# Memory-recurrent attention with an FFN: token-stationary passes of 32 slots, weights streamed in four column groups

## The chip, the cores and the metric

The kernel runs on one core of a Trainium2 chip. The metric is the device time of one execution in microseconds (us), and lower is better. A program on one core is called "fast" when its run lies within 1.5% of the fastest run of the same kernel; a kernel that was run only once has the state "unknown".

The engines are named as in the profile: PE is the matmul engine (PEld its weight loads, which overlap with it), DVE the vector engine, ACT the scalar engine, POOL the general one, SP the one that issues most transfers. A "pair" is one weight load and the matmul that uses it. The stationary operand is the one that the weight load puts into the array; the other one moves through it.

## The reference

A sequence of 2048 tokens of width 640 is normalised and goes through attention in 64 segments of 32 tokens. Each segment attends to itself and to 8 memory slots, and the memory's own outputs are the memory of the next segment. An FFN with a hidden width of 1728 follows, both with residuals. There are 32 heads of width 128, and all data is bf16.

```python
mem = mem0                                   # 8 x 640
for s in range(64):                          # S = 2048, seg_len = 32
    xs = x[:, s * 32:(s + 1) * 32, :]        # x is layernormed
    h = concatenate([mem, xs], axis=1)       # 40 tokens
    q, k, v = (einsum('btd,dhe->bhte', h, W) for W in (Wq, Wk, Wv))      # 32 heads of 128
    scores = einsum('bhqe,bhke->bhqk', q, k) * scale
    scores = where(mask, scores, -1e9)       # mask[q, k] = (q < 8) or (q >= k)
    o = einsum('bhqk,bhke->bhqe', softmax(scores), v)
    o = einsum('bhte,hed->btd', o, Wo)
    mem = o[:, :8, :]                        # the recurrence
    outs.append(o[:, 8:, :])
h = x + concatenate(outs, axis=1)
gate, up = LN(h) @ W_gate, LN(h) @ W_up
return h + ((relu(gate) * up) @ W_down)      # cut: casts
```

By the mask the 8 memory queries see all 40 keys, and the token queries see the memory and the tokens up to their own.

## The kernel before

Everything in the recurrence is feature-major: the weights are stationary, and the 40 tokens of a segment (8 memory slots and 32 tokens) move. One head's projection is five pairs of 128 x 128 weights and 40 moving columns.

```python
for kind, payload in pe_ops:                       # (cut) the program of PE for one segment
    if kind == "tile":                             # 96 of them: V, Q, K of 32 heads
        ...
        for c in range(DC):                        # DC = 5
            mm = pe.matmul(outap, Wqkvv[:, j, c, h * Dh:(h + 1) * Dh], abuf[:, c, :],
                           start=(c == 0), stop=(c == DC - 1))
    ...                                            # "tg" transposes V, "sg" scores and mask,
    ...                                            # "sumpv" sums by a matmul with ones, and PV
    elif kind == "wo":                             # 160 pairs: output projection
        for pair in pairs:
            for h in range(H):
                ...
                for c in pair:
                    mm = pe.matmul(outap, Wov[:, h, c * 128:(c + 1) * 128],
                                   oTv[:, h * L:(h + 1) * L], start=(h == 0), stop=(h == H - 1))
```

The memory of the next segment is copied straight from the output projection's accumulators into the next segment's input, because the layout is the same:

```python
v.tensor_copy(anext[:, 0:5:2, 0:M], memE)
v.tensor_copy(anext[:, 1:5:2, 0:M], memO).then_inc(s_actrdy.h, 1)
```

The start-up loads x transposed, and only then the weights. It normalises all of x and stores it in a scratch buffer in device memory, from where each segment loads its tokens. At the end, the hidden state goes through scratch a second time before the FFN.

```python
def sync_start(sp):
    for b in range(NBLK):
        for c in range(DC):
            sp.dma_start(xT_blk[b][:, c, :], x_ap[b * TB:(b + 1) * TB, c * 128:(c + 1) * 128],
                         transpose=True).then_inc(s_x.h, 16)
def pool_weights(pool):
    pool.wait_ge(s_x.h, X_ALL)
    ...                                            # Wv, Wq, Wk, Wo, 5 MB each
def sync_store_pack(sp, b=b, c_pack_done=c_pack_done):
    sp.wait_ge(s_dln.h, c_pack_done)
    dst = scr_in[b * NSB:(b + 1) * NSB, :, :].rearrange("s p f -> p s f")
    ...
```

The softmax here doesn't subtract the row's maximum and nothing guards it: scores larger than these inputs give would overflow.

## Time and profile before

The median of the first three runs was 2047.39 us (2047.12 to 2047.9). The head of the profile's page gives the span, the busy time of each engine with its share and its count of instructions, and, for the queue that brings the engines' instructions, packets, megabytes and share of the transfer engines' time:

```profile
span 2047.5 us, 101764 instructions
PE 1771.0 (86%) x48661; PEld 1513.0 (74%) x48661; DVE 434.1 (21%) x927; ACT 653.1 (32%) x1185; POOL 8.0 (0%) x17
q8 instruction: 383, 6.28, 1.2%
```

The next view gives the busy times by stretches that I chose: start-up, recurrence, the passage to the FFN, and the FFN. Its columns are the stretch, its length, the busy time and count of each engine, the mean clock that the throttle granted to PE (1 is full speed), and the transfers' share and rate.

```profile
core 0: us, PE busy (x) PEld busy (x) DVE busy (x) ACT busy (x) POOL busy (x), PEclk, DMA share, GB/s
0.00:118.00 118.00, 15.99 (x45) 4.61 (x45) 28.51 (x69) 20.73 (x21) 7.96 (x17) 0.67 0.68 245
118.00:1755.00 1637.00, 1537.80 (x47488) 1409.27 (x47488) 326.19 (x702) 579.20 (x1088) 0.00 (x0) 0.93 0.05 9
1755.00:1796.00 41.00, 8.52 (x20) 2.33 (x21) 8.44 (x23) 7.91 (x7) 0.00 (x0) 0.55 0.74 227
1796.00:2047.00 251.00, 208.65 (x1110) 96.81 (x1108) 70.92 (x133) 45.30 (x69) 0.00 (x0) 0.94 0.03 11
```

Four fifths of the time is the recurrence, and PE is busy for 94% of it, with 742 matmuls a segment (47488 / 64) in 25.6 us. The timeline of one segment, cut to four lines, shows what these are. Its columns are start, duration from the first start to the last end, engine, line and operation, operands, sizes, and the count of instructions that were merged into the line; in brackets stands an idle time just before, and what ended it.

```profile
1000.50 1.69 PE L574 MATMUL ps_all<-act_70,Wqkv 128*128 128x40 bf16 x60
1008.23 4.93 PEld L650 LDWEIGHTS ps_all<-oTs,Wo_sb 128*128 128x128 bf16 x160
1008.23 5.03 PE L650 MATMUL ps_all<-oTs,Wo_sb 128*128 128x40 bf16 x160
1013.92 2.70 PE L574 MATMUL ps_all<-act_71,Wqkv 128*128 128x40 bf16 x100 [0.66 <-DVE act_71 L716]
```

Sixty pairs take 1.69 us, of which 0.18 us is the last matmul's own duration (the mean of one in the profile's groups), so 1.51 us / 59, about 26 ns a pair; 160 take 5.03 us, or 30 ns a pair. The wait for the hand-over of the memory is 0.66 us in the last line. Going by the FFN's matmuls of 512 columns, 0.215 us each, 40 columns would need about 17 ns (an estimate), less than a pair takes. PE is therefore bound by the number of pairs, each with few moving columns.

The chain of waits, in order of time, shows two places outside the recurrence. Its columns are start, duration and what it was:

```profile
41.80 41.54 DMA scr_in<-pack
1755.95 21.71 DMA hTb_85<-scr_h
```

The first store of normalised x to scratch lasted 41.5 us, beside the weights' loads, and the loads of the hidden state for the FFN came 21.7 us after the recurrence.

### The profile page before, as it was taken

Reading aid. Unit: us, or ns where it says so; the run is one execution under the profiler, and the core shown is the slowest. Engines: PE = TensorE matmul, PEld = TensorE weight load, DVE = VectorE, ACT = ScalarE, POOL = GpSimd, SP = SyncE. Lnnn points to the kernel's source line nnn. Section 1 sums busy time; section 2 is a strip of 40 time slices with the busy share of each in tenths; the row PEclk is TensorE's granted clock in tenths of the full one; section 3 lists DMA queues with packets and bytes.
Section 4 is the critical chain, followed back from the end, with each engine's and each line's share of the span. In section 5 each row is a group of like instructions: output and inputs, shape, how many; then the busy total and the mean of one; then the engine's idle time right before and its main releaser. Section 6 shows DMA issues by size and latency. Waiting matters only on the chain.

```text
span 2047.5 us, 101764 instructions
## 1 busy us (share of the span) xinstructions
PE 1771.0 (86%) x48661; PEld 1513.0 (74%) x48661; DVE 434.1 (21%) x927; ACT 653.1 (32%) x1185; POOL 8.0 (0%) x17
## 2 busy tenths in 40 slices
PE   2069999999999999999999999999999999387898
PEld 0068888888888888888888888888888888233344
DVE  1221111122111112222111111111111111133222
ACT  2123333333333333333333333333333333231111
POOL 1000000000000000000000000000000000000000
PEclk8579999999999999999999999999999999688999
DMA  6720000000000000000000000000000000500000
GB/s 215 302 55 9 8 9 9 8 9 9 9 8 9 9 9 8 9 9 8 9 9 9 9 9 9 8 9 9 9 9 9 9 8 8 170 13 13 14 13 14
DMA packets 96619, 55.11 MB, mean 27 GB/s; under 512 B 80008, under 2 KB 91984, under 8 KB 94288
## 3 DMA queue, kind: packets, MB, share of 16 engines
q1 hardware_dynamic: 91136, 26.98, 5.7%
q0 software_dynamic: 3008, 20.97, 2.5%
q8 instruction: 383, 6.28, 1.2%
q10 hardware_dynamic: 2064, 0.66, 0.1%
q14 instruction: 28, 0.23, 0.0%
HBM read 35.48 MB, written 10.49 MB: 22 GB/s over the span
## 4 chain that ended last, share of the span: by engine, by line
PE 79%; ACT 6%; DVE 5%; issue 4%; DMA 4%; SPq 1%; ACTq 0%; DVEq 0%
PE ps_all L574 41%; PE ps_all L650 14%; PE ps_all L589 7%; PE ps_all L979 3%; PE ps_all L982 3%; DMA scr_in<-pack 3%; PE ps_all L1048 3%; PE ps_all L603 3%; ACT L_sb L520 3%; PE ps_all L620 2%; PE ps_all L606 2%; ACT E_sb L510 1%; PE ps_all L629 1%; SPq L291 1%; DMA hTb_85<-scr_h 1%
## 5 line engine op out<-in xcount | busy, mean ns | idle before, releaser
L502 ACT ACTIVATE qkvT<-ps_all 128x480 bf16<-128x480 f32 x512 | 291.2, 569 | 849.6 <-PE ps_all L574 844.2
L574 PE MATMUL ps_all<-act_70,Wqkv 128*128 128x40 bf16 x15360 | 432.9, 180 | 40.4 <-DVE act_70 L716 20.3
L574 PEld LDWEIGHTS ps_all<-act_70,Wqkv 128*128 128x128 bf16 x15360 | 406.3, 96 | 71.6 <-issue 34.0
L574 PE MATMUL ps_all<-act_71,Wqkv 128*128 128x40 bf16 x15360 | 431.9, 180 | 20.9 <-DVE act_71 L716 20.9
L574 PEld LDWEIGHTS ps_all<-act_71,Wqkv 128*128 128x128 bf16 x15360 | 405.4, 96 | 52.2 <-DVE act_71 L716 24.3
L650 PE MATMUL ps_all<-oTs,Wo_sb 128*128 128x40 bf16 x10240 | 323.0, 192 | 1.8
L650 PEld LDWEIGHTS ps_all<-oTs,Wo_sb 128*128 128x128 bf16 x10240 | 312.8, 105 | 7.7 <-DVE oTs L698 5.2
L688 DVE COPY vtok<-ps_all 40x1024 bf16<-40x1024 bf16 x256 | 174.8, 683 | 459.4 <-PE ps_all L589 459.4
L698 DVE TENSOR_TENSOR oTs<-ps_all,r_sb 128x480 bf16<-128x480 f32 (+1 forms) x192 | 115.7, 603 | 615.9 <-ACT r_sb L528 615.9
L589 PE MATMUL ps_all<-ident,qkvT 128*40 128x128 bf16 x2048 | 160.1, 221 | 0.0
L510 ACT ACTIVATE E_sb<-ps_all 40x480 bf16<-40x480 f32 (+1 forms) x192 | 98.7, 514 | 135.2 <-PE ps_all L606 135.2
L520 ACT ACTIVATE L_sb<-ps_all 128x480 f32<-128x480 f32 (+1 forms) x192 | 100.6, 524 | 74.7 <-PE ps_all L620 74.7
L589 PEld LDWEIGHTS ps_all<-ident,qkvT 128*40 128x40 bf16 x2048 | 116.0, 99 | 9.4
L620 PE MATMUL ps_all<-E_sb,ones_bf 40*128 40x480 bf16 (+1 forms) x192 | 68.7, 358 | 54.7 <-ACT E_sb L510 51.5
L528 ACT ACTIVATE r_sb<-L_sb 128x480 bf16<-128x480 f32 (+1 forms) x192 | 107.2, 558 | 6.1
L629 PEld LDWEIGHTS ps_all<-E_sb,vtok 40*128 40x128 bf16 x2048 | 80.1, 94 | 13.8
L603 PE MATMUL ps_all<-qkvT 128*40 128x40 bf16 x2048 | 84.2, 181 | 0.0
L629 PE MATMUL ps_all<-E_sb,vtok 40*128 40x40 bf16 x2048 | 83.2, 178 | 0.0
L620 PEld LDWEIGHTS ps_all<-E_sb,ones_bf 40*128 40x128 bf16 x192 | 17.8, 93 | 77.5 <-ACT E_sb L510 75.1
L603 PEld LDWEIGHTS ps_all<-qkvT 128*40 128x40 bf16 x2048 | 64.3, 97 | 7.6
L606 PE MATMUL ps_all<-mask_bf,ident 40*40 40x480 bf16 (+1 forms) x192 | 68.0, 354 | 0.0
L1048 PE MATMUL ps_all<-Wd_sb,gT 128*128 128x512 bf16 x224 | 52.8, 380 | 14.6 <-DVE outsb_108 L1079 7.9
(126 smaller groups left out, 569.9 us busy)
## 6 DMA issues: line engine op xcount, KB each, us to landing
Wqkv<-in_A_Wv_dram POOLq DMA_DIRECT2D x1, 5120.0 KB, 15.7
Wqkv<-in_A_Wq_dram POOLq DMA_DIRECT2D x1, 5120.0 KB, 27.9
Wqkv<-in_A_Wk_dram POOLq DMA_DIRECT2D x1, 5120.0 KB, 40.5
Wo_sb<-in_A_Wo_dram POOLq DMA_DIRECT2D x1, 5120.0 KB, 54.0
scr_in<-pack SPq DMA_DIRECT2D x4, 1280.0 KB, 5.7
Wg_sb<-in_B_W_gate_dram SPq DMA_DIRECT2D x1, 2160.0 KB, 15.2
Wu_sb<-in_B_W_up_dram SPq DMA_DIRECT2D x1, 2160.0 KB, 21.0
Wd_sb<-in_B_W_down_dram SPq DMA_DIRECT2D x1, 2080.0 KB, 9.5
```

Source lines behind the costliest of these rows:

```text
L502: acte.activation(dst, bank(B_QKV[f % 2])[:, 0:12 * L], ACTF.Copy).then_inc(s_qkvevac.h, 1)
L510: acte.activation(Ev[0:L, goff[g]:goff[g] + ng * L], bank(B_ST)[0:L, 0:ng * L], ACTF.Exp, scale=SCALE).then_inc(s_exp.h, 1)
L520: acte.activation(Lv[:, 0:ng * L], bsum[:, 0:ng * L], ACTF.Ln).then_inc(s_ln.h, 1)
L574: mm = pe.matmul(outap, Wqkvv[:, j, c, h * Dh:(h + 1) * Dh], abuf[:, c, :], start=(c == 0), stop=(c == DC - 1))
L589: mm = pe.matmul(bank_bf(B_TR)[0:L, jj * Dh:(jj + 1) * Dh], qkvTv[:, tV(h), :], ident[:, :], is_transpose=True)
L603: pe.matmul(bk[0:L, i2 * L:(i2 + 1) * L], qkvTv[:, tK(h), :], qkvTv[:, tQ(h), :], start=(i2 == 0), stop=False)
L620: pe.matmul(bsum[:, 0:ng * L], ones_bf[0:L, :], Ev[0:L, goff[g]:goff[g] + ng * L], start=True, stop=True).then_inc(s_sumfill.h, 1)
L629: mm = pe.matmul(bpv[:, i2 * L:(i2 + 1) * L], vtokv[0:L, h * Dh:(h + 1) * Dh], Ev[0:L, h * L:(h + 1) * L], start=True, stop=True)
L650: mm = pe.matmul(outap, Wov[:, h, c * 128:(c + 1) * 128], oTv[:, h * L:(h + 1) * L], start=(h == 0), stop=(h == H - 1))
L688: v.tensor_copy(vtokv[0:L, NHB * G * Dh:(NHB * G + NHB) * Dh], bank_bf(B_TR)[0:L, 0:NHB * Dh]).then_inc(s_vtevac.h, 1)
L698: v.tensor_tensor(oTv[:, goff[g]:goff[g] + ng * L], bpv[:, 0:ng * L], rv[:, goff[g]:goff[g] + ng * L], ALU.mult).then_inc(s_oready.h, 1)
L1048: pe.matmul(b6[:, 0:512], gTv[0:nf, j, u * 128:(u + 1) * 128], Wd_sb[0:nf, j, 0:512], start=(j == 0), stop=False)
```

## The change

The idea is to exchange the roles of weights and tokens. The activations become stationary, 32 slots at a time, and the weights move 512 columns at a time, in four column groups of 32: matmuls of different groups write different quarters of the partitions, so that four may run beside one another.

- A pass of the recurrence has 32 slots: the 8 memory slots of its segment and 24 tokens of later segments, so that no slot is empty. The tokens' keys, queries and values go into ring buffers that the later segments read. 64 segments have 2048 tokens, 64 passes carry 1536, and the left-over ones (32 of each 128) get extra passes in three steps of four. The first two segments' tokens are projected ahead of the loop.
- The attention of the tokens (scores_x, pv_x) stands beside the recurrence: it fills PE while ACT and DVE work for the memory.
- Softmax sums come from a column of ones in V, and reciprocals from DVE, instead of matmuls with ones and two ACT passes; masks are applied by a minimum after the exponential.
- The way through scratch at the start is gone, because the activations are transposed on PE. Attention outputs still go to device memory (attn_d) and come back in the FFN.
- The FFN comes last as before; its weights take the place of the projection weights, and are loaded after the recurrence. Its layernorms (ln2) are done block by block inside the loop.

The new kernel is written anew, so the diff is cut to its core:

```diff
-                    for c in range(DC):
-                        mm = pe.matmul(outap, Wqkvv[:, j, c, h * Dh:(h + 1) * Dh], abuf[:, c, :],
-                                       start=(c == 0), stop=(c == DC - 1))
+    def qkv_bank(act, akeys, j, i, dst, dkey, eng):
+        ...
+            for c in range(DC):
+                for g in range(4):
+                    o = 2048 * i + 512 * g
+                    ins = pe.matmul(bank(b)[32 * g:32 * g + 32, :], act[:, c, :], W[:, j, c, o:o + 512],
+                                    start=(c == 0), stop=(c == DC - 1), skip_group_check=True)
 ...
-                                mm = pe.matmul(outap, Wov[:, h, c * 128:(c + 1) * 128],
-                                               oTv[:, h * L:(h + 1) * L],
-                                               start=(h == 0), stop=(h == H - 1))
+    def wo_pass(src, keys, bk, dst, dkey, eng, halves=(0, 1)):
+        ...
+                for hb in range(16 * hf, 16 * hf + 16):
+                    ...
+                    for gg in range(4):
+                        i = pe.matmul(bank(bk)[32 * gg:32 * gg + 32, 0:160], src[:, hb, :], w[:, gg],
+                                      start=(hb == 0), stop=(hb == 31), skip_group_check=True)
 ...
+    def scores_mem(s):                              # 64 pairs of 8 columns; scores_x: 64 of 32
+        ...
+            for k in range(8):
+                for g in range(4):
+                    pe.matmul(bank(BM)[32 * g:32 * g + 32, k * 8:k * 8 + 8], KmT[:, 4 * k + g, :],
+                              QmT[:, 4 * k + g, :], start=True, stop=True, skip_group_check=True)
+                for g in range(4):
+                    i = pe.matmul(bank(BM)[32 * g:32 * g + 32, 64 + k * 8:64 + k * 8 + 8],
+                                  Kr[:, 4 * k + g, p:p + 32], QmT[:, 4 * k + g, :], ...)
 ...
+    ld_init = ln1_load(-1)                          # x rows of the first two segments
+    for j in (1, 0, 2):
+        for i in range(2):
+            dma(W[:, j, :, 2048 * i:2048 * i + 2048], ...)
+    dma(Wo[:, :, :], A_Wo.rearrange("h e d -> e h d"), w=[("Wo",)])
+    ln1(-1, ld_init, XP0)
+    ln1(0, ln1_load(0), XP1)                        # x rows that the first pass needs too
 ...
+        if not last:
+            scores_mem(s)
+            if units:
+                units[0]()                          # left-over tokens, first half
+            ...
+            pv_mem(s)
+        scores_x(s)
+        if len(units) > 1:
+            units[1]()                              # left-over tokens, second half
+        ...
+        wo_pass(oT[par], [("oT", par, "m"), ("oT", par, "x")], BM, wtok[par], ("wtok", par), "dve")
+        if not last:
+            to_act(s + 1, ("wtok", par), wtok[par]) # the memory of the next step
+        ...
+        pv_x(s)
 ...
+            if b + 1 < NBLK and j in (2, 4, 6, 8):  # in the FFN, between its matmuls
+                ln2(4 * (b + 1) + (2, 4, 6, 8).index(j), BT[j // 2 % 2])
```

Each `add` names what an operation reads and writes, and a small solver puts in the semaphores; each engine carries out its operations in the order in which they are added.

## The prediction

> **What bounds it now.** Three stages (busy time by stretches): start-up to about 118 us (matmuls busy 27.6 of the first 130 us; the chain of waits shows a 41.5 us store to scratch behind the weight loads), 64 recurrent segments to 1755 us, the FFN to 2047 us. In the recurrence PE is busy 94%; the timeline gives 25.55 us a segment of some 770 matmuls, each with its own weight load: 60 projection matmuls of 40 columns take 1.69 us, 160 output-projection ones 5.03 us, that is (less the last one's latency) 26 and 30 ns a pair. [...]the segment is bound by the rate at which weight-load/matmul pairs issue. About 2-3 us a segment is exposed waiting.
>
> **The change.** Activations become stationary (8 memory slots, 24 later tokens); weights stream 512 columns at a time into four column groups. Projection pairs fall from 480 to 120 a step, plus 40 in three steps of four for left-over tokens. x attention is pushed to later steps and fills PE while ACT/DVE work for the memory. The Ln/Exp reciprocals, sums and mask matmuls go. Start-up no longer goes through scratch. The FFN gets deeper buffers and loses the identity residual matmuls.
>
> **A step on PE (estimate).** The Trainium skill, "TensorE: Matmul & The Clock Gate" (Packing small matmuls), says column groups run concurrently and measured 2.38x for three. No trace here shows that yet. The FFN's 512-column matmuls run at 1.08 us per five, 0.215 each; with four at once a projection bank of 20 costs 1.07 us.
> - 6 banks 6.4 us, left-over ones 1.6
> - about 26 transposes at 64 ns (as this trace's): 1.7
> - memory scores 64 pairs, x scores 64, memory PV 16, x PV 64, at 27 ns: 5.6
> - output projection 128 pairs, plus 32 on average for left-over tokens, at 27-30 ns: 4.5
>
> Sum 19.8 us. I add 2.5 us for switching tile shapes ("TensorEngine Tiling", Key Properties, says a switch drains TensorE; not shown here) and unfilled waits: **22.3 us a step** against 25.55. The gain is modest because the small pairs stay at the issue rate. DVE (about 9 us a step) and ACT (about 6) stay off the bound.
>
> **Sum.** First step done at about 70 us (weights arrive by 55-65 us), 63 x 22.3 = 1405 -> 1475. Tail about 30 us: three output projections, then FFN weights (6.4 MB, issued only after the last stores) and four layernorms. FFN 56 x 2.15 + 32 x 1.9 = 182, about 190 with block changes. Total **1690 us**, 80% range 1540 to 1840. Faster by over 2%: 0.90; within 2%: 0.03; slower: 0.07.
>
> **What would show it.** In the timeline: (1) a projection bank of 20 matmuls in 1.1 us (4.3 us without overlap). (2) Scores, PV and output projection at 26-30 ns a pair. (3) Steps every 21-24 us, PE over 88% busy, gaps below 1 us. (4) First step over by about 70 us. (5) About 220 us from the last step to the end.
>
> **What would make it wrong.** Column groups that overlap only in part (0.3 us more a bank adds 2.3 us a step, 145 us in all; no overlap makes it slower than before). Weight loads not hidden in tiled shapes. Larger drains at shape switches. Tiled pairs issuing faster than 26 ns would save up to 4 us a step. A memory chain (exp, min, PV, reciprocal, transpose, output projection, hand-over) that the filling work does not cover. DMA issue on one queue delaying value rows.

## The result

The changed kernel took 1563.79 us (median of four, 1555.93 to 1566.89) against 2047.64 (2047.12 to 2048.27). The ratio is 0.7633, with a 95% interval of 0.7613 to 0.7652; the result is correct. Ratios here and below are computed as the mean time of one kernel's fast runs over that of the other's of the same rounds, so they are not quite the ratio of the medians that I quote. The profiled run is the shortest of the four, with a span of 1554.2 us.

```profile
span 1554.2 us, 77215 instructions
PE 1275.4 (82%) x36507; PEld 809.4 (52%) x36507; DVE 632.3 (41%) x1687; ACT 415.6 (27%) x736; POOL 4.1 (0%) x21
q8 instruction: 285, 4.67, 1.3%
```

The stretches below are again start-up with the first step, recurrence, the passage to the FFN, and the FFN:

```profile
core 0: us, PE busy (x) PEld busy (x) DVE busy (x) ACT busy (x) POOL busy (x), PEclk, DMA share, GB/s
0.00:102.00 102.00, 32.88 (x740) 19.50 (x744) 16.83 (x49) 11.84 (x20) 4.14 (x21) 0.98 0.57 213
102.00:1242.00 1140.00, 1014.72 (x34301) 675.79 (x34288) 528.98 (x1468) 349.96 (x610) 0.00 (x0) 0.99 0.10 19
1242.00:1291.00 49.00, 12.73 (x412) 10.53 (x412) 8.95 (x24) 5.68 (x14) 0.00 (x0) 0.59 0.50 171
1291.00:1554.00 263.00, 215.10 (x1068) 103.53 (x1068) 77.52 (x148) 48.08 (x93) 0.00 (x0) 0.92 0.08 24
```

The recurrence gained about 500 us. The other three stretches together took 414 us against 410 (118 + 41 + 251) before, so the parts that the change was also meant to shorten did not get shorter. The last row is the clearest sign: PE has 1068 instructions there against 1110, and is busy for 215 us of 263.

### A step of the recurrence

The first matmul of the second step's projections starts at 102.4 us and that of the last step at 1230.0 us, which is 62 intervals of 18.19 us. The timeline of one of them, cut to some lines of PE and its weight loads:

```profile
701.91 4.50 PE L330 MATMUL ps<-W,act_r_66 128*32 128x512 bf16 x80
706.24 1.25 PE L350 MATMUL ps<-W,act_r_66 128*32 128x512 bf16 x20
709.51 0.18 PE L466 MATMUL ps<-QmT,KmT 128*32 128x8 bf16 x4
709.54 0.18 PE L469 MATMUL ps<-QmT,Kr 128*32 128x8 bf16 x4
...
714.28 2.25 PE L514 MATMUL ps<-Wo,oT_87 128*32 128x160 bf16 x118
717.35 0.18 PEld L514 LDWEIGHTS ps<-Wo,oT_87 128*32 128x32 bf16 x10 [1.02 <-issue]
717.35 0.39 PE L514 MATMUL ps<-Wo,oT_87 128*32 128x160 bf16 x10 [0.82 <-issue]
```

The 80 matmuls of four banks run from 701.91 until the next bank starts at 706.24, so a bank of 20 takes 1.08 us. In the FFN five matmuls of the same width start 1.08 us apart from the next five, so one takes 0.215 us by itself, and 20 in series would take 4.3 us. Four column groups run side by side without a loss that shows. The two lines of scores, four pairs each, start 0.03 us apart, so about 8 ns a pair. The output projection's 118 pairs end at 716.53 and take 17 ns each. Then there is a pause of about a microsecond inside the projection, before 10 more pairs of the same kind. The profile puts that pause down to "issue", which means that PE waited for nothing that the profile shows. I return to it.

The mean over 40 steps, by phase (time from a phase's first start to the next phase's first start, so pauses are in it):

```text
phase                                     us a step   pairs    ns a pair   predicted us
projections (4 banks Q/K, 2 banks V)      4.45+2.33   80+40    56-58       6.4
left-over tokens' banks                   1.19+0.61   (mean)               1.6   (sum 8.6)
transposes                                2.46        30                   1.7
scores_mem                                0.54        64        8.4        1.7
scores_x                                  0.83        64       12.9        1.7
pv_mem                                    0.28        16       17          0.4
pv_x                                      1.73        64       27          1.7
output projection (step, left-over mean)  2.81+0.90   128+32   22-28       4.5
```

The rows add up to 18.1 of the step's 18.2 us. Where no pause falls into a phase, scores_x took 0.51 us (8 ns a pair), pv_x about 0.95 us (15 ns), and the output projection 17 ns a pair. Adding up the phases without the pauses gives about 15.5 us; the pauses marked "issue" of over 0.4 us come to 1.81 us a step (64 of them in 40 steps), and waits for other engines of over 0.4 us to 0.91 us a step. Here and below the 40 steps are the last ones before the final step, and a pause is measured from the start of the matmul before it to the start of the one after it.

### Start-up

The next lines are of the timeline of the changed kernel's start, cut:

```profile
8.30 0.55 SPq L298 DMA_DIRECT2D xt<-in_A_x_dram  x1
...
30.59 6.20 SPq L298 DMA_DIRECT2D Wo<-in_A_Wo_dram  x1
36.91 20.98 SPq L298 DMA_DIRECT2D xt<-in_A_x_dram  x1
65.39 0.89 DVE L302 BATCH_NORM_STATS2 st<-xt 128x6 f32<-128x320 bf16 x2 [51.47 <-DMA xt<-in_A_x_dram]
68.34 4.46 PE L330 MATMUL ps<-W,act_r_67 128*32 128x512 bf16 x40
```

Two loads of x rows go to the same buffer xt. The first one is issued at 8.30 us, ahead of the weights. The second one, 160 KB, stands in the same queue behind 21 MB of weights, and DVE waits 51.47 us for it. In PE's order the transposes of these rows stand ahead of the first projection, which so starts at 68.34 us.

### The passage to the FFN

The timeline of the changed kernel from the last step to the FFN's first matmul, cut:

```profile
1240.50 0.41 SPq L298 DMA_DIRECT2D Wg<-in_B_W_gate_dram  x1
1250.15 1.01 PE L514 MATMUL ps<-Wo,oT_88 128*32 128x160 bf16 x46 [3.02 <-issue]
1274.69 0.37 SPq L298 DMA_DIRECT2D xt_0_98<-in_A_x_dram  x1
1277.96 0.49 DVE L603 TENSOR_TENSOR h_0_106<-xt_0_98,at_100 128x640 bf16<-128x640 bf16 x1 [26.44 <-DMA at_100<-attn_d]
```

The FFN's weights are issued at 1240.50 us and later, the rows of x and attention for its first layernorm only at 1274.69, on the same queue behind them, and DVE waits 26.44 us for these. The FFN's first matmul starts at 1291.29. Three output projections of 128 pairs each run from 1242.67 to 1257.6, which is 39 ns a pair. Two things are in this figure: pauses of 3.02 and 2.15 us in which nothing is waited for, and the granted clock. The pairs start 17 ns apart until 1251.2 us, at a granted clock of 1.00, and 33 ns apart from then on, where the clock was 0.52 (1251.0 to 1257.6 us).

### The FFN

The timeline of the changed kernel in the FFN: five matmuls in the usual course, then the place where a layernorm for the next block falls.

```profile
1367.72 1.24 PE L776 MATMUL ps<-xn2T_115,Wg 128*128 128x512 bf16 x5
1373.01 0.45 DVE L308 TENSOR_SCALAR xt_0_98<-h_0_106,mv,rs 128x640 bf16<-128x640 bf16 x1 [0.67 <-ACT rs L307]
1373.51 0.45 PE L314 MATMUL ps<-ident,xt_0_98 128*128 128x128 bf16 x5 [3.47 <-DVE xt_0_98 L308]
1373.80 2.05 PE L776 MATMUL ps<-xn2T_115,Wg 128*128 128x512 bf16 x5
```

PE reaches the five transposes of the next block's rows before DVE has normalised these rows. It keeps to the order of the program here, so it idles for 3.47 us although the next gate matmuls need nothing from the layernorm. The five matmuls after it take 2.05 us instead of 1.24, at a lower granted clock (0.62 from 1373.5 to 1376.0 us; the mean is 0.92 in the FFN and 0.99 in the recurrence).

### The profile page after: what moved, and what is told of

Same layout as the page of the kernel before. It is cut to its first block, busy times and chain, and to the rows that moved or that the text cites. A ratio compares the mean times of both kernels' runs of the same rounds, so it can differ in the third digit from the quotient of the medians.

```text
span 1554.2 us, 77215 instructions
## 1 busy us (share of the span) xinstructions
PE 1275.4 (82%) x36507; PEld 809.4 (52%) x36507; DVE 632.3 (41%) x1687; ACT 415.6 (27%) x736; POOL 4.1 (0%) x21
## 3 DMA queue, kind: packets, MB, share of 16 engines
q8 instruction: 285, 4.67, 1.3%
## 4 chain that ended last, share of the span: by engine, by line
PE 74%; DVE 9%; issue 7%; DMA 4%; ACT 3%; SPq 3%; POOL 0%; DVEq 0%; POOLq 0%
PE ps L330 23%; PE ps L514 12%; PE ps L350 10%; PE ps L776 9%; PE ps L564 5%; PE ps L798 4%; PE ps L364 4%; SPq L298 3%; DVE tok_73 L337 2%; DMA xt<-in_A_x_dram 2%; DVE st L302 2%; PE ps L535 1%; PE ps L532 1%; PE ps L490 1%; PE ps L314 1%
## 5 line engine op out<-in xcount | busy, mean ns | idle before, releaser
L330 PE MATMUL ps<-W,act_r_67 128*32 128x512 bf16 x2680 | 154.9, 383 | 2.7 <-DVE rx L575 1.4
L330 PE MATMUL ps<-W,act_r_66 128*32 128x512 bf16 x2560 | 148.9, 384 | 2.4 <-issue 2.3
L335 ACT ACTIVATE tok_70<-ps 128x512 bf16<-128x512 f32 x65 | 38.8, 597 | 354.6 <-PE ps L330 354.6
L330 PEld LDWEIGHTS ps<-W,act_r_67 128*32 128x32 bf16 x2680 | 69.8, 97 | 74.2 <-DVE tok_71 L337 6.6
L514 PE MATMUL ps<-Wo,oT_88 128*32 128x160 bf16 x4224 | 88.2, 239 | 21.4 <-issue 16.1
L330 PEld LDWEIGHTS ps<-W,act_r_66 128*32 128x32 bf16 x2560 | 67.7, 97 | 71.5 <-issue 8.4
L337 DVE CAST tok_73<-ps 128x512 bf16<-128x512 f32 x92 | 63.6, 692 | 99.5 <-PE ps L330 97.4
L577 DVE TENSOR_TENSOR ox<-ps,rx 128x384 bf16<-128x384 f32 (+1 forms) x192 | 98.5, 513 | 6.6
L514 PE MATMUL ps<-Wo,oT_87 128*32 128x160 bf16 x4224 | 83.2, 236 | 13.2 <-DVE oT_87 L380 10.6
L514 PEld LDWEIGHTS ps<-Wo,oT_88 128*32 128x32 bf16 x4224 | 77.0, 99 | 30.7 <-issue 20.6
L335 ACT ACTIVATE tok_72<-ps 128x512 bf16<-128x512 f32 x92 | 54.9, 597 | 122.6 <-PE ps L330 122.6
L350 PE MATMUL ps<-W,act_r_67 128*32 128x512 bf16 x1360 | 85.6, 380 | 0.0
L514 PEld LDWEIGHTS ps<-Wo,oT_87 128*32 128x32 bf16 x4224 | 74.3, 98 | 21.2 <-DVE oT_87 L380 15.9
L350 PE MATMUL ps<-W,act_r_66 128*32 128x512 bf16 x1280 | 81.0, 380 | 0.0
L337 DVE CAST tok_71<-ps 128x512 bf16<-128x512 f32 x65 | 45.0, 692 | 67.7 <-PE ps L330 67.7
L378 ACT ACTIVATE Kr<-ps 128x768 bf16<-128x768 bf16 (+3 forms) x74 | 52.4, 724 | 44.8 <-DVE KmT L380 43.4
L532 PE MATMUL ps<-Qr,Kr 128*32 128x32 bf16 x2048 | 46.6, 180 | 10.9 <-issue 10.9
L378 ACT ACTIVATE Qr<-ps 128x768 bf16<-128x768 bf16 (+3 forms) x74 | 52.1, 723 | 1.5 <-PE ps L364 1.5
```

The lines of the kernel that those rows point to most:

```text
L330: ins = pe.matmul(bank(b)[32 * g:32 * g + 32, :], act[:, c, :], W[:, j, c, o:o + 512], start=(c == 0), stop=(c == DC - 1), skip_group_chec ...
L335: add("act", lambda a: a.activation(dst, bank(b), ACTF.Copy), r=[B(b)], w=[dkey])
L337: add("dve", lambda v: v.tensor_copy(dst, bank(b)), r=[B(b)], w=[dkey])
L350: ins = pe.matmul(bank(b)[32 * g:32 * g + 32, :], act[:, c, :], W[:, 2, c, o:o + 512], start=(c == 0), stop=(c == DC - 1), skip_group_chec ...
L378: add("act", lambda a: a.activation(dst, src, ACTF.Copy), r=r, w=w)
L514: i = pe.matmul(bank(bk)[32 * gg:32 * gg + 32, 0:160], src[:, hb, :], w[:, gg], start=(hb == 0), stop=(hb == 31), skip_group_check=True)
```

## The experiments

### The theories

The prediction's number was within its range, but its parts were not. Four questions were tested.

- G, for the column groups: that four matmuls run side by side when four consecutive ones go to four different groups. Its rival is that their order does not matter, because the cheapness comes from the shape alone.
- F, for instruction fetch: the recurrence runs at the rate at which PE's instructions come in, so that the pauses marked "issue" are waits for instructions. The trace holds the packets of the instruction queue. The changed kernel has 285 of them, 4.67 MB in all, so 16 KB each. They carry about 256 of PE's instructions (128 pairs) each, come 4.3 to a step, and never start less than 3.3 us apart (median 3.9). After the pauses of over 0.4 us in 40 steps, PE's next instruction starts 1.38 us (median) after such a packet ended, and 90% of them lie between 1.24 and 1.52 us (of moments picked at random in these steps, 7% lie there). Three of them, as read from the trace:

```text
packet start + took      its end      pause of PE
698.16 + 1.34            699.50       699.44 to 700.86
714.92 + 1.16            716.08       716.30 to 717.35
728.49 + 0.88            729.37       729.28 to 730.88
```

- R, the rival of F: the pauses have another cause that does not depend on how many instructions there are, such as the switch between shapes, and a further pair costs only the 8 to 9 ns that the timeline shows. The Trainium skill's page "Runtime: NRT & Kernel Launch", section Instruction fetch mechanics, speaks for R: it says that instructions come in blocks of 16 KiB or 256 instructions, which this trace shows too, and that crossing to the next block is mostly hidden.
- And the three stretches outside of the steady steps: that the order of issue on the transfer queue (start, passage) and on PE (FFN) costs what the timeline says.

In the expectations, "G", "F" and "R" are these. Each experiment is an edit of the changed kernel, except where said. All gave correct results.

### e1: the column groups one after the other

```diff
-            for c in range(DC):
-                for g in range(4):
+            for g in range(4):
+                for c in range(DC):
                     o = 2048 * i + 512 * g
                     ins = pe.matmul(bank(b)[32 * g:32 * g + 32, :], act[:, c, :], W[:, j, c, o:o + 512],
```

> Only the order of the projection matmuls changes: group by group (g outside, c inside) instead of the four groups in turn. Same instructions, same result. Theory (the gain comes from four column groups streaming at once): five matmuls that follow each other sit in one group and wait for each other, so a bank of 20 goes from 1.08 us to about 3.7 us (only the seams between groups overlap) and the kernel to 2750-3150 us, slower than the kernel before. Rival (the gain comes from having fewer matmuls, not from groups streaming at once): no change, about 1560 us.

Measured: 1724.94 us in a single run (state unknown), so slower than the change by 161 us, but far from what I had expected. A bank took 1.38 us (68.9 ns a pair) instead of 1.08, and nothing like 3.65 us, which is my estimate of a strict order (17 starts at 0.215 us, because three of the 20 can overlap with the group before). This was a miss. Either the order of groups hardly matters, or PE does not start matmuls strictly in the order of the program: one of a free column group may start before an earlier one whose group is busy. e9 and e10 tell these apart.

### e2: 64 more small pairs

The scores of the memory are computed twice; the second time overwrites the first with the same values.

```diff
-            for k in range(8):
+            for k in [q % 8 for q in range(16)]:
                 for g in range(4):
                     pe.matmul(bank(BM)[32 * g:32 * g + 32, k * 8:k * 8 + 8], KmT[:, 4 * k + g, :],
```

> The 64 memory-score pairs of every step are issued twice (same result, 8 columns each). Theory F (PE runs out of fetched instructions in bursts of short pairs; gaps of 0.8-1.7 us with nothing waited for, 1.8 us a step): the step needs half a 16 KB fetch more, so it costs 1.0-1.8 us a step, 63 to 113 us in all, and those gaps grow to about 3 us a step. Rival R (the gaps have another cause): 64 pairs at 8.4 ns, 0.54 us a step, about 34 us in all, gaps unchanged.

Measured: 1685.79 us (1678.9 to 1688.53), ratio 0.8228 (0.8209 to 0.8246), which is 122 us more than the change. A step took 20.12 us instead of 18.21, so 1.91 us for 64 pairs, or 30 ns a pair, although the timeline shows these pairs starting 8 to 9 ns apart. The rest went into longer and more frequent pauses: 3.31 us a step instead of 1.81. There were 4.775 packets of instructions a step instead of 4.3.

### e3: the scores by column group

The 16 pairs of one column group are issued in a row, then those of the next group; the count of pairs is the same.

```diff
-            for k in range(8):
-                for g in range(4):
+            for g in range(4):
+                for k in range(8):
                     pe.matmul(bank(BM)[32 * g:32 * g + 32, k * 8:k * 8 + 8], KmT[:, 4 * k + g, :],
                               QmT[:, 4 * k + g, :], start=True, stop=True, skip_group_check=True)
 ...                                                # the same in scores_x
```

> Scores issued group by group instead of the four groups in turn; same instructions. Theory G (the 26 ns of a pair is a floor for pairs that follow each other in one column group, and pairs in different groups overlap below it): memory scores from 8 to about 26 ns a pair, x scores from 13 to about 26, so 1.7-2 us a step more on PE; with theory F most of today's 1.8 us of fetch gaps vanish behind it, net 20 to 75 us slower. Rival 1 (order of groups does not matter for short pairs): no change. Rival 2 (G without F): 110-126 us slower, gaps unchanged.

Measured: 1604.23 us, ratio 0.7831 (0.7813 to 0.7848), 40 us more than the change. The scores took 21.4 and 23.0 ns a pair instead of 8.4 and 12.9, and a step 18.99 us. The pauses went down to 1.17 us a step: while PE was held up by the array, instructions could come in. So a pair that follows one in its own column group costs over 20 ns, near the 26 ns of the kernel before, and the cheapness of small pairs comes from alternating groups.

### e4: the scores of memory and tokens in one pair

The queries of the memory are stored in front of the tokens' ones, so that one matmul of 40 columns does what two of 8 and 32 columns did. This makes 64 pairs fewer in a step, with the same arithmetic.

```diff
-                    pe.matmul(bank(BM)[32 * g:32 * g + 32, k * 8:k * 8 + 8], KmT[:, 4 * k + g, :],
-                              QmT[:, 4 * k + g, :], start=True, stop=True, skip_group_check=True)
+                    pe.matmul(bank(BM)[32 * g:32 * g + 32, k * QS + lo:k * QS + QS], KmT[:, 4 * k + g, :],
+                              Qr[:, 4 * k + g, a + lo:a + QS], start=True, stop=True, skip_group_check=True)
 ...                                                # QS = 40; scores_x is gone
```

> Memory queries stand beside the 32 x queries of the same step, so one matmul of 40 columns makes both scores: 64 pairs fewer in each step (about 561 to 497). Theory F: a half fetch less and 0.5 us less issue, 1.2-1.8 us a step, 75 to 115 us faster than the changed kernel; gaps fall well below 1.8 us a step. Rival R: 0.5 us a step, about 32 us faster, gaps unchanged.

Measured: 1470.85 us (1469.26 to 1477.47), ratio 0.7192 (0.7173 to 0.7211), 93 us less than the change. The merged scores take 0.54 us (8.4 ns a pair), so 0.83 us less than the two groups together took, but a step lost 1.38 us (16.83 us) and its pauses went down to 1.11 us.

The lines of the profile that carry the verdict are the packets of instructions (the page) and the pauses in front of the output projection's weight loads (the view of waits, whose columns are the total in us, the number and the longest one). First the changed kernel, whose packets were shown above:

```profile
PEld ps L514 <- issue: 39.8, 42, 3.2
```

Then both lines of e2:

```profile
q8 instruction: 317, 5.19, 1.3%
PEld ps L514 <- issue: 61.4, 62, 3.7
```

And both of e4, where the output projection is line 537:

```profile
q8 instruction: 254, 4.16, 1.2%
PEld ps L537 <- issue: 27.1, 29, 2.9
```

The output projection has the same pairs in all three kernels, and yet its pauses grow and shrink with the count of instructions elsewhere. R allows 32 to 34 us for 64 pairs more or fewer; the runs showed 122 and 93, where F allowed 63 to 113 and 75 to 115. F holds, and e2 was a little dearer than F's range: its extra pairs cost nearly the full 30 ns that the packets' pace gives (3.9 us for 128 pairs). That PE could merely issue no more than so many pairs a microsecond, with no fetch in it, does not fit the pauses: pairs start 8 ns apart, and then PE stops for about a microsecond until some 1.4 us after a packet. e2 is the cleaner of the two, because e4 also moves the tokens' scores to an earlier place and the memory's PV to another accumulator bank.

### e5: the rows of x ahead of the weights

The first load gets its own buffer, so that the second one need not wait for it and can be issued before the weights.

```diff
     ld_init = ln1_load(-1)
+    ld_0 = ln1_load(0)
 ...                                                # the loads of the weights
     ln1(-1, ld_init, XP0)
-    ln1(0, ln1_load(0), XP1)
+    ln1(0, ld_0, XP1)
```

> The load of the x rows of the first pass is issued before the 21 MB of weights instead of behind them (its first 64 rows get a buffer of their own). Theory: the first pass waits for x, not for weights; the first projections start at about 25 us instead of 68, the second step's projections at about 70-75 instead of 102, the kernel is 25-32 us faster. Rival (the weights themselves hold the start back, x only lands with them): under 8 us.

Measured: 1532.51 us (1527.11 to 1538.82), ratio 0.7495 (0.7466 to 0.7523), 31 us less. The second step's projections start at 73.3 us instead of 102.4. In e5's timeline PE's first projection now waits for a weight instead of for x, and starts at 18.91 us instead of 68.34:

```profile
18.91 6.31 PE L331 MATMUL ps<-W,act_r 128*32 128x512 bf16 x60 [2.13 <-DMA W<-in_A_Wk_dram]
```

### e6: the FFN's transposes later than its layernorms

The vector part of the layernorm stays where it is in the order; PE's transposes are issued two column blocks of the FFN later.

```diff
             gate_up(b, j)
+            if b + 1 < NBLK and j in (4, 6, 8, 10):
+                ln2_t(4 * (b + 1) + (4, 6, 8, 10).index(j), BT[j // 2 % 2])
             if b + 1 < NBLK and j in (2, 4, 6, 8):
-                ln2(4 * (b + 1) + (2, 4, 6, 8).index(j), BT[j // 2 % 2])
+                ln2(4 * (b + 1) + (2, 4, 6, 8).index(j), None)
```

> In the FFN the transposes of a normalised tile are put two gate/up groups later on PE than its layernorm; nothing else changes. Theory: PE, in order, waits 3.5 us at each of 12 tiles and its clock drops after it; FFN falls from 263 to 195-205 us, kernel 50-70 us faster, granted clock in the FFN above 0.95. Rival (DVE and ACT work of the layernorm delays the evictions, wherever the transposes stand): under 20 us.

Measured: 1503.13 us (1497.06 to 1504.53), ratio 0.7336 (0.732 to 0.7351), 61 us less than the change. The FFN went down from 263 to 202 us. In e6's timeline the transposes follow the matmuls without a wait, and the five matmuls after them take the usual 1.24 us:

```profile
1366.76 0.44 PE L314 MATMUL ps<-ident,xt 128*128 128x128 bf16 x5
1367.04 1.24 PE L781 MATMUL ps<-xn2T,Wg 128*128 128x512 bf16 x5
```

The view by stretches has this row for e6's FFN, to be compared with the last row of that view of the changed kernel:

```profile
1299.00:1501.00 202.00, 195.53 (x1068) 99.64 (x1068) 77.50 (x148) 46.80 (x93) 0.00 (x0) 0.99 0.10 32
```

The twelve waits of about 3.5 us account for some 42 us of the gain. The clock, 0.99 in place of 0.92, would account for about the rest: with 215 us of busy time in one and 195.5 in the other for the same instructions, it is 20 us.

### e7: the passage to the FFN in another order

On top of e6, the FFN's weights go to POOL's queue and are issued within the last step, the rows for the first layernorms are issued before the last output projections, and the last transposes are mixed with those.

```diff
+    def ffn_w01():
+        dma(Wg[:, :, :], B_W_gate.rearrange("(c p) f -> p c f", p=128), w=[...], eng="pool")
+        dma(Wu[:, :, :], B_W_up.rearrange("(c p) f -> p c f", p=128), w=[...], eng="pool")
 ...
+        if last:
+            ffn_w01()
 ...
+    ln2(0, None)
+    ln2(1, None)
     trans_ox(NSEG - 1, T1)
+    tail_wo(NSEG - 2)
+    ln2_t(0, BT[0])
+    ln2(2, None)
+    tail_wo(NSEG - 1)
```

> On top of e6: FFN weights are loaded on the GpSimd queue, gate and up during the last step; the first four layernorms stand before and between the last output projections. Theory: of the 49 us between the last step and the FFN about 15 remain (the output projections), so 25-35 us faster than e6; the instruction fetches at the end, 4.7-6.5 us apart beside the weight loads, come back to 3.6 us. Rival (output projections alone set the tail): under 8 us.

Measured: 1482.41 us (1480.98 to 1487.47), ratio 0.7245 (0.7231 to 0.7258), 21 us less than e6. I had expected 25 to 35, so this is a small miss. The last step with the passage went from 60.8 to 39.7 us. What stays is, first, a chain that the new order does not take away: the attention rows must be stored and loaded again, then normalised (PE waits 6.68 us for DVE once). Second, the output projections take 4.43, 4.04 and 2.40 us, at granted clocks of 0.52, 0.58 and 1.00. Third, the slow instruction packets have only moved. In the changed kernel's passage they came 5.5 to 6.8 us apart while the weights were loaded. In e7 the loads fall into the last step, and there the packets come 4.9 to 6.4 us apart and PE pauses:

```profile
1257.71 0.23 PE L568 MATMUL ps<-Vp,Px 8*32 8x129 bf16 x2 [3.46 <-issue]
```

After the loads two of the three packets come 3.7 to 3.8 us apart, as had been expected; in the interval of 6.8 us PE also waits 2.69 us for DVE. That the loads slow the packets fits this, but no run tested it alone.

### e8: the second left-over bank after the output projection

This moves a slow stretch (few instructions, much array time) between the output projection and pv_x, both of which use many instructions.

```diff
         scores_x(s)
-        if len(units) > 1:
-            units[1]()
 ...
             store_attn(wtok[par], ("wtok", par), M, 32 * (s - 2), RID)
+        if len(units) > 1:
+            units[1]()
         pv_x(s)
```

> The second left-over projection bank (20 slow pairs) moves from before the output projection to between it and the x PV, that is into the longest run of short pairs; same instructions. Theory F: the pause in demand falls where the buffer is empty, so gaps fall by 0.3-0.8 us a step, 15 to 45 us faster. Rival (that bank covers the reciprocal and multiply of the memory PV, and its loss is felt there): 10-40 us slower. Both may act and cancel.

Measured: 1562.21 us (1560.08 to 1567.56), ratio 0.7634 (0.7619 to 0.7649): no difference from the change's 0.7633. The pauses were 1.90 us a step against 1.81. Neither expectation came true, and the run decides nothing. A possible reading, which I did not test, is that the count of instructions in a step is the same, so that the time that is missing is only moved to another place.

### e9 and e10: sixteen more matmuls, in one group or in all

These follow from the miss in e1. Every projection bank gets 16 more matmuls of 512 columns in front, which the real ones overwrite afterwards. In e9 all 16 go to the first column group, in e10 they go round all four.

```diff
+            for n in range(16):
+                g = (0, 0, 0, 0)[n % 4]             # e10: (0, 1, 2, 3)
+                o = 2048 * i + 512 * g
+                pe.matmul(bank(b)[32 * g:32 * g + 32, :], act[:, 0, :], W[:, j, 0, o:o + 512],
+                          start=True, stop=True, skip_group_check=True)
             for c in range(DC):
                 for g in range(4):
```

> Each projection bank gets 16 more 512-column matmuls ahead of its 20, all in column group 0 (overwritten by the real ones, same result). The first run of this study that only reordered groups could not decide. Theory ([...]four groups run at once, and PE may start a later matmul of a free group first): group 0 has 21 matmuls of 0.215 us, a bank takes about 4.5 us, about 25 us a step more, kernel 2900-3300 us. Rival (a 32-column matmul is simply four times as fast in whichever group): 16 x 0.054 us more a bank, the same as its twin run, about 1950-2050 us.

> The same 16 more matmuls a bank, four in each group. Theory and rival agree here: a bank of 36 in 36 x 0.054 = 1.94 us, 6.5 us a step more, kernel 1950-2050 us. Only the difference from the twin run tells the theories apart.

Measured, in single runs of unknown state: 3175.13 us and 1941.76 us. The step took 43.07 us in e9 and 23.98 us in e10. In e9 a bank took 4.53 us from its start to the next bank's, which is (16 + 5) x 0.216 us: the busiest group decides. In e10 a matmul took 54 to 56 ns, a quarter of 0.215 us. The same count of instructions thus costs four times less when they are spread over the groups.

The timeline of e9 also shows the order. Line 330 is the extra matmuls, line 335 the real ones, which stand after all of line 330 in the program:

```profile
1505.25 0.40 PE L335 MATMUL ps<-W,act_r 128*32 128x512 bf16 x3
1505.46 0.38 PE L330 MATMUL ps<-W,act_r 128*32 128x512 bf16 x1
1505.48 0.39 PE L335 MATMUL ps<-W,act_r 128*32 128x512 bf16 x3
1505.68 0.38 PE L330 MATMUL ps<-W,act_r 128*32 128x512 bf16 x1
```

Three real matmuls start, then an extra one that precedes them in the program, then three more, and the last extra one. So a matmul of a free column group does start ahead of earlier ones whose group is busy, but only over a short distance: 14 of the 16 extra ones had started by the first line. Each time three waiting matmuls of group 0 are overtaken and no more, at first the last two extra ones and the first real one. That would explain e1, where the next group's matmuls can start while some of the group before are still waiting. Whether three is a limit in other programs too was not measured.

### e11: all repairs together

This has the edits of e4, e5, e6 and e7, and a split of the tokens' first layernorm (which comes once in four steps) like that in e6, with its vector part ahead of the transposes:

```diff
+    def ln1_norm(b, n):
+        norm_rows(xt, ("xt",), n, xt, ("xt",))
-    def ln1(b, n, bk):
+    def ln1(b, n, bk, norm=True):
```

> The x load first, merged scores, later FFN transposes, FFN weights on another queue and the tail reordered, all as tried one by one; new: the layernorm of the next x block is computed two projections before its transposes (its 1.1 us wait, once in four steps, about 15 us in all). If the gains add (93 + 31 + 60 + 21 + 15): about 1340 us, 1325 to 1365. If they overlap (stalls that move elsewhere): above 1380.

Measured over five rounds: 1360.27 us (1357.52 to 1366.67), ratio 0.6653 (0.664 to 0.6665). It beats both kernels, with 203.5 us less than the change, and lies in the expected range. The single gains of the runs above, 93 + 31 + 61 + 21, and 15 expected for the split, which was not run alone, add up to 221, so most of them are independent. The page of its profile:

```profile
span 1355.8 us, 69206 instructions
PE 1213.5 (90%) x32475; PEld 769.1 (57%) x32475; DVE 630.5 (47%) x1687; ACT 406.3 (30%) x757; POOL 7.8 (1%) x25
```

PE is busy for 90% of the span (82% before the repairs). The second step starts at 72.3 us, a step takes 16.7 to 16.8 us with pauses of 1.01 us, and the FFN takes 202 us.

## Why the prediction was right or wrong

The forecast was 1690 us with a range of 1540 to 1840, and the kernel took 1563.79, in the range and 126 us below the forecast. The direction was right, and so was the mechanism behind it, four column groups at once. That the sum came so near, however, was luck: its errors had different signs. With the profiled run's span, by stretch:

```text
                                            predicted   measured   difference
second step's projections start                 70        102.4       +32
62 further intervals (of 22.3, of 18.19)      1383       1128        -255
last step and passage, to the FFN's start       52         61.3        +9
FFN                                            190        263         +73
sum                                           1695 *     1554       -141
* rounded to 1690 in the prediction
```

The steps, as the prediction put them:

- "with four at once a projection bank of 20 costs 1.07 us": right. It is 1.08 us. Check (1) held.
- "memory scores 64 pairs, x scores 64, memory PV 16, x PV 64, at 27 ns: 5.6" and "output projection 128 pairs, plus 32 on average for left-over tokens, at 27-30 ns: 4.5": wrong, and the main failure. I took 26 to 30 ns a pair from the kernel before, where every pair uses the whole array. Over four column groups a pair takes 8 ns in the scores, about 15 in pv_x and 17 in the output projection. The two terms come to about 2.3 and 3.0 us without pauses, so 4.8 us less. e3 shows the reason: with the groups in a row the same scores cost 21 to 23 ns a pair. I had named this in the list of what could make the prediction wrong ("Tiled pairs issuing faster than 26 ns would save up to 4 us a step"), and it is what happened. Check (2) failed.
- "I add 2.5 us for switching tile shapes ... and unfilled waits": the size was right and the cause was not. The steps have 1.81 us of pauses without a wait and 0.91 us of waits for other engines. A switch of shape costs little: from a bank to the transposes the first start comes 0.31 us after the last one, against 0.21 us between the starts within a bank, and at the other switches (from the transposes to a bank, from the output projection to pv_x, from pv_x to a bank) the excess is about 0.1 us too. With some 6.5 switches a step that is about 0.65 us, an estimate. The pauses come from instruction fetch, as e2 and e4 show. A packet, that is 128 pairs, came every 3.3 us at best and every 3.9 us in the median, which is 26 and 30 ns a pair on the mean of all pairs that PE runs. The figure that I had used for each small pair is therefore real as a mean over a longer stretch, and it is not paid where wide matmuls stand nearby: the banks (120 pairs in 6.8 us, 56 ns each) run slower than instructions come in, and so can let the fetch get ahead.
- "Steps every 21-24 us, PE over 88% busy, gaps below 1 us": the step was 18.2 us, PE was busy for 89% (1014.72 of 1140 us), and the pauses were mostly 0.85 to 1.7 us each. One of the three was right.
- "First step done at about 70 us (weights arrive by 55-65 us)": wrong by 32 us. I looked at when the weights arrive, and not at what stood behind them in the same queue. "DMA issue on one queue delaying value rows" was on my list of risks, for another load. e5 gives 31 us back.
- "Tail about 30 us: three output projections, then FFN weights ... and four layernorms": 49 us. The loads of the first layernorm's rows stood behind 6.4 MB of weights. e7 gives 21 us back, about as much as the term was short of (19 us).
- "FFN 56 x 2.15 + 32 x 1.9 = 182, about 190 with block changes": 263 us. The matmuls were costed to within some 12 us (e6 runs the FFN in 202 us), but I took it that removed identity matmuls and deeper buffers would leave PE without waits, and did not follow PE's order through the layernorms. With the tail, check (5) expected 220 us from the last step to the end, and it was 312 (1242 to 1554).

Some things stay open. Before the change, PE's pairs run at an even 26 ns, and the packets there also come at least 3.35 us apart (median 4.15, some 254 instructions each). I found no pause of over 0.4 us marked "issue" in it between 300 and 1600 us. Whether the 26 ns are the array's own pace or the fetch's was not tested. The projections' starts lie 25 to 26 ns apart without a lump, which speaks for the array's own pace, because the fetch shows itself in lumps in the changed kernel; but the two figures are too near to be sure without a run of that kernel with other pairs. The order in e8 was tested and gave no answer. And what fraction of e2's extra cost is due to a lower chance of hiding later fetches was not separated.

## What to carry to other kernels

When a kernel is cut into many small matmuls, cost two things separately: what the array needs for each, which falls with alternating column groups (by four for 512 columns, from over 20 to 8 ns for the memory's scores), and what all instructions together need to come in (here 3.9 us for 128 pairs), which is a budget over some microseconds. Where the second is the tighter one, merging pairs pays more than the timeline of these pairs shows. Follow every in-order queue, transfers and PE alike, past the operation that you cost, to the one that stands behind it: three such places cost this kernel 113 us together (31, 61 and 21), at no change of the work. A forecast whose sum is right says little about its parts, so check them by stages.

## What the Trainium skill lacked or had wrong

- "Runtime: NRT & Kernel Launch", Instruction fetch mechanics: it calls the crossing of a 16 KiB block mostly hidden. The block's size agrees with the traces (4.67 MB in 285 packets). But for PE with small pairs the fetch is not hidden: pauses of 0.85 to 1.7 us, 1.81 us in a step of 18.2, each ending about 1.4 us after a packet; 64 more pairs in a step cost 122 us and 64 fewer saved 93. The section gives no rate; here packets came at least 3.3 us apart (median 3.9).
- "TensorE: Matmul & The Clock Gate", Wait — 56ns, not 53.3ns?: it says that starts are never less than about 25 ns apart, however narrow the matmul. That agrees with pairs of the whole array before the change (26 ns) and nearly with pairs of one column group in a row (21 to 23 ns in e3). It does not hold across column groups: 64 pairs started 8.4 ns apart. Its Part 3 (Packing small matmuls) measures 2.38x for three groups. Four groups gave 4x here (20 matmuls in 1.08 us, 0.215 us each alone). That part also says that matmuls start and end strictly in program order; in e9 matmuls of free groups started before an earlier one of a busy group, and e1's banks took 1.38 us, not the 3.65 us of a strict order.
- "TensorEngine Tiling (Array Packing)", Key Properties: it says that a change of mode drains the engine, without a size. Here a switch cost about 0.1 us, to the transposes (0.31 us between starts in place of 0.21) and at the other switches of a step.
